# Attention and routed experts: transposes by row halves, and scores of the next pair ahead of back products

## The chip, the cores and the metric

The kernel runs on one core of one Trainium2 chip. Its engines are TensorE (PE, with its weight loads shown apart as PEld), VectorE (DVE), ScalarE (ACT), GpSimd (POOL) and SyncE (SP, which issues most transfers). The metric is the device time of one execution in microseconds, lower is better. Three executions of the kernel before took 696.68, 697.42 and 697.74 us; the median is 697.42 us.

## What is computed

Block-causal attention for 8 batches of 8 heads, 576 positions and 64 features, and behind it a layer of 8 experts, of which each token uses one:

```
scores = (q @ k.T) / 8             # per batch and head
mask   = row // 64 >= column // 64 # blocks of 64 positions
attn   = softmax(where(mask, scores, -1e9))
x      = (attn @ v)                # heads side by side: 4608 tokens x 512
logits = x @ w_gate + modality_bias[modality_id]
e      = argmax(logits);  gate = softmax(logits)[e]
out    = gate * (relu(x @ w1[e]) @ w2[e])
```

## The kernel before

**Tiling.** Two heads of one batch make a pair; there are 32 pairs. The features of the two heads lie on partitions 0 to 63 and 64 to 127, so that a matmul of one head uses one half of the rows of the PE array. The 576 query rows of a head are nine strips of 64; strip s sees 64(s+1) columns. The work of a pair is cut into named steps, and `emit` (called from `run_slot`) writes a step's instructions:

- `Q` (`scale`): queries times 1/8. `S0` to `S3` (`scores`): the strips' scores into PSUM banks 0 to 5, both heads in one bank. S0 is strip 7 in bank 0, S1 strips 6 and 0 in bank 1.
- `M0` to `M4` (`maxima`): negated row maxima on DVE, for strips (7), (6, 0), (5), (4, 2) and (3, 1, 8). `E0` to `E4` (`exps`): exponentials with row sums on ACT, into the tile `pm`.
- `T0` to `T5` (`transposes`): `pm` is turned on PE, 23 blocks of 128 columns with both heads at once, four blocks to a bank. `C0` to `C5` (`copies`): the banks are copied into `pt`, 0, 1 and 5 by DVE, the others by ACT.
- `V` (`values`): value products into banks `o0` and `b0`. `O` (`turn_out`): ACT copies them out to `ot`. `D` (`inverse`): denominators on DVE (`den`, then a reciprocal).
- `B` (`back`): products that turn the result back to rows and add the router's logits, into `o0` and `b0` again. `Z0`, `Z1` (`rows`): DVE scales them into records (`xr`, `gl`), Z0 from `o0`, Z1 from `b0`.
- `L`: SP loads a later pair's queries and keys.

**Order.** Nothing is scheduled by a planner. The table `ORDER` lists (step, stage); in turn `slot` the step is written for pair `slot - stage`, each engine executes in the order of writing, and semaphores are derived from the tiles' uses. A turn is one pass through `ORDER`. The loop is a pipeline: scores, exponentials and transposes of one pair run together with the value and back products of the pair before it. `LAST` is the list for the final pair.

**Routing.** After each fourth pair (a batch) a list of 20 small steps computes where the batch's tokens go. The `q` entries of `ORDER` pop from that list; most are DVE steps. Two are PE matmuls into `b0` (`total`, `counts`, popped at `qp`), and two are ACT copies of those tables out of `b0` (popped at `qv`). At `M3`, `V` and `B` (`SPOTS`) a scatter of records can be written: an index on DVE (L395) and an indirect transfer on POOL. From turn 19 on POOL also splits expert weights there (a CAST and a subtraction, L591 and L592).

**Experts.** Behind attention, from about 290 us on, PE runs the experts' matmuls; the change doesn't touch them.

The array: a matmul takes a stationary operand, loaded first, and streams a moving one. In a transpose the data is stationary and an identity is the moving operand:

```
pe.transpose(banks[g][0:m, 128 * i : 128 * i + 128], d.pm[:, o : o + m], idf)
```

## Time and profile before

| | |
|---|---|
| median of three executions | 697.42 us |
| profiled execution, time | 696.26 us |
| profiled execution, span | 694.5 us |
| PE busy | 685.5 us (99%) |
| PEld busy | 568.8 us (82%) |
| DVE, ACT, POOL busy | 381.3, 352.0, 187.1 us |
[...]

The span is what the profiler saw of the profiled execution; 1.76 us of its time lie around it. A busy time is the union of an engine's instructions. Matmuls are pipelined, so PE can be shown busy and still wait for a moment; a stage's length is read from the starts of its matmuls. Attention takes the first 290 us of the span, the experts the rest.

### The profile page before, as it was taken

The numbers are of one execution on the slowest core, as the hardware profiler recorded it, in microseconds if no ns is written. First come the engines' busy times: TensorE is split into PE (matmuls) and PEld (weight loads), VectorE is DVE, ScalarE is ACT, GpSimd is POOL, SyncE is SP. The second block draws the span as 40 slices with busy tenths as digits, with TensorE's granted clock in tenths as the row PEclk, the third lists the DMA queues.
The fourth block names the chain that finished last, engine by engine and source line by source line (L and its number), as shares of the span: only waits on it lengthen the run. The fifth ranks groups of instructions, "written<-read, shape, count | busy, mean of one in ns | idle before, by whom it ended". The sixth has DMA issues, their size and how long they took to land. (4 is left out here: it accounts for less than half of the span.)

```text
span 694.5 us, 17615 instructions
## 1 busy us (share of the span) xinstructions
PE 685.5 (99%) x6856; PEld 568.8 (82%) x6856; DVE 381.3 (55%) x1090; ACT 352.0 (51%) x1023; POOL 187.1 (27%) x234
## 2 busy tenths in 40 slices
PE   8999999999999999999999999999999999999996
PEld 5888888888888878988888888888888888888885
DVE  6888989999999999883142323223132132322121
ACT  6889899989999898422141322313123032231221
POOL 4000031335275773699311300302002020020201
PEclk9999999999999999999999999999999999999999
DMA  6343354557555763423662520504408040020200
GB/s 223 119 120 117 120 161 145 166 166 220 149 189 212 218 215 114 95 81 113 120 142 92 118 65 1 121 1 105 135 1 242 1 106 15 1 83 1 70 22 19
DMA packets 48070, 76.47 MB, mean 110 GB/s; under 512 B 9710, under 2 KB 30574, under 8 KB 47984
## 3 DMA queue, kind: packets, MB, share of 16 engines
q1 hardware_dynamic: 41456, 55.81, 29.6%
q0 software_dynamic: 6528, 19.50, 7.8%
q8 instruction: 55, 0.90, 0.5%
q14 instruction: 31, 0.25, 0.1%
HBM read 54.19 MB, written 21.27 MB: 109 GB/s over the span
## 5 line engine op out<-in xcount | busy, mean ns | idle before, releaser
L745 DVE SCALAR_TENSOR_TENSOR extra<-bank,extra 128x512 fp32r<-128x512 f32 (+1 forms) x72 | 47.6, 662 | 234.5 <-ACT extra L744 234.5
L229 ACT ACTIVATE pm<-bank,nm 128x512 f32<-128x512 f32 (+3 forms) x320 | 156.0, 502 | 22.8 <-DVE nm L216 22.3
L744 ACT ACTIVATE extra<-bank 128x512 fp32r<-128x512 f32 (+1 forms) x72 | 41.4, 575 | 214.8 <-PE bank L741 214.8
L216 DVE TENSOR_REDUCE nm<-bank 128x1 f32<-128x512 f32 (+3 forms) x320 | 120.5, 446 | 0.7 <-PE bank L209 0.7
L396 POOL DMA_INDIRECT records<-xr,pi x72 | 73.0, 1014 | 174.9 <-DVE pi L395 70.2
L236 PE MATMUL bank<-cf,pm 128*128 128x128 f32 (+1 forms) x736 | 88.7, 276 | 1.9 <-ACT pm L229 1.8
L209 PE MATMUL bank<-raw 64*64 64x512 f32 (+7 forms) x1280 | 87.5, 406 | 0.0
L236 PEld LDWEIGHTS bank<-cf,pm 128*128 128x128 f32 (+1 forms) x736 | 78.6, 139 | 9.0 <-ACT pm L229 7.3
L209 PEld LDWEIGHTS bank<-raw 64*64 64x64 f32 x1280 | 54.6, 133 | 27.9 <-issue 21.5
L259 PE MATMUL b<-pt,v 64*64 64x64 f32 (+1 forms) x868 | 72.7, 265 | 0.0
L259 PE MATMUL o<-pt,v 64*64 64x64 f32 (+1 forms) x868 | 67.2, 261 | 0.0
L241 DVE COPY pt<-bank 128x512 f32<-128x512 f32 (+1 forms) x96 | 58.7, 637 | 14.9 <-PE bank L236 6.5
L229 ACT ACTIVATION_READ_ACCUMULATOR pm<-bank,nm 128x1 f32 x320 | 65.3, 204 | 0.0
L741 PE MATMUL bank<-extra,w0ha 128*128 128x512 f32 (+1 forms) x192 | 62.4, 356 | 0.0
L741 PE MATMUL bank<-extra,w0la 128*128 128x512 f32 (+1 forms) x160 | 58.8, 368 | 0.0
L259 PEld LDWEIGHTS b<-pt,v 64*64 64x64 f32 (+1 forms) x868 | 53.1, 136 | 2.4
L850 POOL DMA_INDIRECT out<-scratch,ids_b x9 | 8.7, 972 | 162.2 <-ACT scratch L849 161.3
L259 PEld LDWEIGHTS o<-pt,v 64*64 64x64 f32 (+1 forms) x868 | 48.4, 135 | 4.4
L241 ACT COPY pt<-bank 128x512 f32<-128x512 f32 x96 | 51.8, 638 | 0.0
L842 PE MATMUL bank<-extra 128*128 128x512 f32 x216 | 50.4, 389 | 0.0
L741 PE MATMUL bank<-xtl,w0ha 128*128 128x512 f32 x128 | 50.0, 390 | 0.0
L741 PE MATMUL bank<-extra,w0hb 128*128 128x512 f32 x128 | 49.8, 389 | 0.0
(235 smaller groups left out, 1147.2 us busy)
## 6 DMA issues: line engine op xcount, KB each, us to landing
raw<-qk SPq DMA_DIRECT2D x31, 576.0 KB, 3.9
v<-vr SPq DMA_DIRECT2D x32, 384.0 KB, 4.0
xr<-records SPq DMA_DIRECT2D x32, 256.0 KB, 5.3
staging<-w SPq DMA_DIRECT2D x32, 128.0 KB, 3.8
staging<-w SPq DMA_DIRECT2D x8, 512.0 KB, 5.0
plain<-w SPq DMA_DIRECT2D x16, 128.0 KB, 6.0
plain<-w SPq DMA_DIRECT2D x4, 512.0 KB, 9.8
records<-bias SPq DMA_DIRECT2D x3, 544.0 KB, 3.5
```

Of the source, the lines that this page charges most:

```text
L209: pe.matmul(place(s, a, b)[64 * t : 64 * t + 64], d.q[hs, D * s : D * s + D], d.k[hs, a:b], start=True, stop=True)
L216: dve.tensor_reduce(d.nm[:, i : i + 1], place(s, a, b), AX.X, ALU.max, negate=True)
L229: act.activation(d.pm[:, o : o + b - a], place(s, a, b), AF.Exp, bias=d.nm[:, s : s + 1], scale=1.0, accum_out=total)
L236: pe.transpose(banks[g][0:m, 128 * i : 128 * i + 128], d.pm[:, o : o + m], idf)
L241: dve.tensor_copy(dst, src) if g in ON_DVE else act.copy(dst, src)
L259: pe.matmul(o.rearrange("p (n c) -> p n c", c=64), d.v[rows, h, block, :], x, start=start, stop=stop)
L396: last = pool.indirect_dma_start(records[:], bass.IndirectOffsetOnAxis(ap=g.pi[i], axis=0), xr[:, i, :], None, bounds_check=2 * NROW - 1, ...
L741: nc.tensor.matmul(hp, w[:, kc, ms], x[:, kc, 0:n], start=i == 0, stop=i == len(mm) - 1)
L744: nc.scalar.activation(hh, hp, AF.Relu)
L745: nc.vector.scalar_tensor_tensor(hl, hp, 0.0, hh, ALU.max, ALU.subtract)
L842: nc.tensor.matmul(y, s.hs[m][x][:, ts], self.part(w, 1, m // 2)[:, m % 2, :], start=first, stop=last)
L850: last = nc.gpsimd.indirect_dma_start(self.out, bass.IndirectOffsetOnAxis(ap=s.list.ids[:, s.t + i : s.t + i + 1], axis=0), yo, None, boun ...
```

## The change

1. **Transposes by halves.** Each of the 23 blocks is turned by two instructions, one for each head: 64 rows of `pm`, 128 columns, against a 64 x 64 identity. Head 0 goes to an even bank and head 1 to the odd bank beside it. There are three groups of 8, 8 and 7 blocks (`GROUPS`) instead of six of four; T0 fills banks 0 and 1, T1 banks 2 and 3, T2 banks 4 and 5. C0 and C1 wait for T0, C2 and C3 for T1, C4 and C5 for T2. A copy moves 512 (C4 and C5: 448) columns and writes runs of 64 into `pt`. The column offsets in `pm` (`OFF`, `TAIL`) are moved so that a half block of strip 2 can be read as a full one. The first group takes blocks of strips 7, 6, 5, 4 and 2.
2. **Order.** S0, S1, M0 and M1 of the next pair are written at the end of a turn, the scores ahead of `B`, the maxima behind it; Z0 and Z1 move from the end of a turn into the next one, Z0 behind M1 and ahead of M2, Z1 behind M2 and ahead of M3. `qv` (the tables' way out) moves behind Z1. `OPENING` writes the first pair's S0, S1, M0 and M1 ahead of the first turn.
3. **Queries.** GpSimd scales the queries of pairs 1 to 17 (`BY_POOL`), where it did pair 1 alone; ACT keeps the later ones.

```diff
--- before.py
+++ after.py
@@ -34,6 +34,7 @@
 COVER = SLOT * NSLOT
 COVER_B = COVER - FEW
 EARLY, NLEAD, LENT = 3, 3, 5
+BY_POOL = 17
 HURRIED = (25, 26, 29, 30, 31)
 LEAD = SLOT * NLEAD
 BIG = float(1 << 20)
@@ -52,14 +53,18 @@
 LONG = (5, 384)
 FLIP = (6, 0, 5, 4, 2)
 PIECES = (((7, 0, 512),), ((6, 0, 448), (0, 0, 64)), ((5, 0, 384), (8, 0, 512)), ((4, 0, 320), (3, 0, 256), (2, 0, 192), (8, 512, 576), (1, 0, 128)))
-OFF = {7: 0, 5: 512, 3: 896, 1: 1152, 6: 1280, 0: 1728, 4: 1792, 8: 2176, 2: 2688}
-TAIL = 2112
+OFF = {7: 0, 5: 512, 3: 896, 1: 1152, 6: 1280, 0: 1728, 2: 1792, 4: 1984, 8: 2368}
+TAIL = 2304
 GROUPS = (
-    ((7, 0), (7, 1), (7, 2), (7, 3)), ((2, 0), (4, 0), (6, 0), (5, 0)), ((3, 0), (3, 1), (6, 2), (5, 2)),
-    ((1, 0), (4, 1), (6, 1), (5, 1)), ((8, 0), (8, 1), (8, 2), (8, 3)), ((6, 3), (4, 2), (2, 1)),
+    ((7, 0), (7, 1), (7, 2), (7, 3), (6, 0), (5, 0), (4, 0), (2, 0)),
+    ((6, 1), (6, 2), (5, 1), (5, 2), (4, 1), (3, 0), (3, 1), (1, 0)),
+    ((6, 3), (4, 2), (2, 1), (8, 0), (8, 1), (8, 2), (8, 3)),
 )
-BLOCK = (12, 0, 8, 4, 16, 20)
-POS = {x: BLOCK[g] + i for g, group in enumerate(GROUPS) for i, x in enumerate(group)}
+ROOMS = (
+    ((2, 0), (4, 0), (6, 0), (5, 0)), ((1, 0), (4, 1), (6, 1), (5, 1)), ((3, 0), (3, 1), (6, 2), (5, 2)),
+    ((7, 0), (7, 1), (7, 2), (7, 3)), ((8, 0), (8, 1), (8, 2), (8, 3)), ((6, 3), (4, 2), (2, 1)),
+)
+POS = {x: 4 * r + i for r, room in enumerate(ROOMS) for i, x in enumerate(room)}
 ON_DVE = (0, 1, 5)
 SUMS = ((2, 4, 6, 5), (1, 3, 7, 8, 0))
 TAILS = ((6, 3, 20, 0), (0, 5, 20, 1), (4, 2, 21, 0), (8, 4, 21, 1), (2, 1, 22, 0))
@@ -69,18 +74,20 @@
 PARTS = (("idf", (128,)), ("ii", (128,)), ("iom8", (NE,)), ("iom72", (NSUB, NE)), ("first9", (NE, NSUB)), ("base8", (NE,)), ("edges", (N // SLOT,)), ("side", (NSUB,)), ("token", (NSUB,)), ("nth", (N // 128,)), ("few", (2,)), ("half", (1,)))
 
 ORDER = (
-    ("S0", 0), ("S1", 0), ("Q", -1), ("M0", 0), ("qv", 1), ("E0", 0), ("S2", 0), ("M1", 0), ("E1", 0), ("S3", 0), ("M2", 0), ("E2", 0), ("M3", 0), ("E3", 0), ("M4", 0),
+    ("Q", -1), ("E0", 0), ("S2", 0), ("Z0", 2), ("M2", 0), ("E1", 0), ("S3", 0), ("Z1", 2), ("qv", 1), ("M3", 0), ("E2", 0), ("M4", 0), ("E3", 0),
     ("L", -2), ("V", 1), ("q1", 1), ("E4", 0), ("O", 1), ("q2", 1), ("q3", 1), ("q4", 1),
-    ("T0", 0), ("C0", 0), ("T1", 0), ("C1", 0), ("D", 1), ("T2", 0), ("C2", 0), ("q5", 1), ("T3", 0), ("C3", 0), ("T4", 0), ("C4", 0), ("T5", 0), ("C5", 0), ("qp", 1), ("B", 1), ("q6", 1), ("Z0", 1), ("Z1", 1),
+    ("T0", 0), ("C0", 0), ("C1", 0), ("D", 1), ("T1", 0), ("C2", 0), ("q5", 1), ("C3", 0), ("T2", 0), ("C4", 0), ("C5", 0),
+    ("S0", -1), ("S1", -1), ("qp", 1), ("B", 1), ("q6", 1), ("M0", -1), ("M1", -1),
 )
+OPENING = ("S0", "S1", "M0", "M1")
 
 SPOTS = ("M3", "V", "B")
 EARLY_STEPS = {
     **{(slot, name): ("prep",) for slot in range(19, 30) for name in SPOTS if (slot, name) != (29, "B")},
-    (18, "S0"): ("chosen",), (18, "V"): ("stage",), (18, "T3"): ("stage",), **{(slot, "T3"): ("restage",) for slot in range(19, 32)}, (20, "L"): ("ids",), (26, "T0"): ("fetch",), (31, "T0"): ("fetch",),
+    (18, "V"): ("chosen", "stage"), (18, "T1"): ("stage",), **{(slot, "T1"): ("restage",) for slot in range(19, 32)}, (20, "L"): ("ids",), (26, "T0"): ("fetch",), (31, "T0"): ("fetch",),
 }
 LAST = (
-    ("+turn0", 0), ("V", 1), ("+place", 0), ("O", 1), ("D", 1), ("+up0", 0), ("+place", 0), ("B", 1), ("Z0", 1), ("Z1", 1), ("+steps1", 0), ("+place", 0), ("+up1", 0),
+    ("Z0", 2), ("Z1", 2), ("+turn0", 0), ("V", 1), ("+place", 0), ("O", 1), ("D", 1), ("+up0", 0), ("+place", 0), ("B", 1), ("Z0", 1), ("Z1", 1), ("+steps1", 0), ("+place", 0), ("+up1", 0),
     ("+place", 0), ("+steps10", 0), ("+place", 0), ("+up2", 0), ("+place", 0), ("+steps9", 0), ("+up3", 0), ("+flush", 0),
 )
 
@@ -185,7 +192,7 @@
         if p == 0:
             for i, j in ((FIRST, S), (0, FIRST)):
                 dve.tensor_scalar(d.q[:, i:j], d.q[:, i:j], SCALE, None, ALU.mult)
-        elif p == 1:
+        elif p <= BY_POOL:
             pool.tensor_scalar(d.q, d.q, SCALE, None, ALU.mult)
         else:
             act.mul(d.q, d.q, SCALE)
@@ -230,15 +237,22 @@
 
     def transposes(p, g):
         d = pairs[p]
-        for i, (s, j) in enumerate(GROUPS[g]):
-            o = OFF[s] + 128 * j
-            m = 64 if s == 2 and j == 1 else 128
-            pe.transpose(banks[g][0:m, 128 * i : 128 * i + 128], d.pm[:, o : o + m], idf)
-
-    def copies(p, g):
+        order = sorted(GROUPS[g], key=POS.get)
+        for s, j in GROUPS[g]:
+            i, o = order.index((s, j)), OFF[s] + 128 * j
+            for h in range(2):
+                hs = slice(64 * h, 64 * h + 64)
+                pe.transpose(banks[2 * g + h][:, 64 * i : 64 * i + 64], d.pm[hs, o : o + 128], idf[hs, hs])
+
+    def copies(p, c):
+        g, h = c // 2, c % 2
         n = len(GROUPS[g])
-        dst, src = pairs[p].pt[:, BLOCK[g] : BLOCK[g] + n].rearrange("p b c -> p (b c)"), banks[g][:, 0 : 128 * n]
-        dve.tensor_copy(dst, src) if g in ON_DVE else act.copy(dst, src)
+        first = min(POS[x] for x in GROUPS[g])
+        dst, src = pairs[p].pt[:, first : first + n, 64 * h : 64 * h + 64], banks[c][:, 0 : 64 * n].rearrange("p (b q) -> p b q", q=64)
+        if g == 0:
+            dst = pairs[p].pt[:, 0:16, 64 * h : 64 * h + 64].rearrange("p (a b) q -> p a b q", b=4)[:, 0:4:3]
+            src = src.rearrange("p (a b) q -> p a b q", a=2)
+        dve.tensor_copy(dst, src) if c in ON_DVE else act.copy(dst, src)
 
     def sides(p):
         return (o0, b0) if p < NPAIR - 1 else (banks[0], banks[1])
@@ -534,6 +548,8 @@
         load(1)
         scale(0)
         load_rest()
+        for name in OPENING:
+            emit(name, 0)
         for slot in range(NPAIR + 1):
             run_slot(slot)
     with tc.manual_schedule(engines=engines):
```

On DVE, at the end of the turn in which the first batch's routing begins (`pt` copies, denominators, then the rows and maxima). Before:

```order
L241 COPY pt1_115<-bank0_97 128x512
L241 COPY pt1_115<-bank1_98 128x512
L286 SCALAR_TENSOR_TENSOR den_851<-sums_635,long0_65 128x9
L287 RECIPROCAL inv_852<-den_851 128x9
L241 COPY pt1_115<-bank5_102 128x384
L299 TENSOR_TENSOR xr1_81<-o0_103,inv_852 128x5x64
L300 TENSOR_TENSOR gl_893<-o0_103,inv_852 128x40
L299 TENSOR_TENSOR xr1_81<-b0_104,inv_852 128x4x64
L300 TENSOR_TENSOR gl_893<-b0_104,inv_852 128x32
L216 TENSOR_REDUCE nm_899<-bank0_97 128x1
L216 TENSOR_REDUCE nm_899<-bank1_98 128x1 x2
L216 TENSOR_REDUCE nm_899<-bank2_99 128x1
```

On DVE, the same place after:

```order
L255 COPY pt1_115<-bank0_97 128x2x4x64
L255 COPY pt1_115<-bank1_98 128x2x4x64
L300 SCALAR_TENSOR_TENSOR den_974<-sums_725,long0_65 128x9
L301 RECIPROCAL inv_975<-den_974 128x9
L255 COPY pt1_115<-bank5_102 128x7x64
L223 TENSOR_REDUCE nm_1012<-bank0_97 128x1
L223 TENSOR_REDUCE nm_1012<-bank1_98 128x1 x2
L313 TENSOR_TENSOR xr1_81<-o0_103,inv_975 128x5x64
L314 TENSOR_TENSOR gl_1049<-o0_103,inv_975 128x40
L223 TENSOR_REDUCE nm_1012<-bank2_99 128x1
L313 TENSOR_TENSOR xr1_81<-b0_104,inv_975 128x4x64
L314 TENSOR_TENSOR gl_1049<-b0_104,inv_975 128x32
```

The rows of a pair (`xr`, `gl`) stood ahead of all maxima (`nm`) and now stand between them.

On PE, in the same turn, from the last transposes to the scores; L323 is the routing table `total`, L280 the back products, L209 the scores. Before:

```order
L236 MATMUL bank5_102<-cf_61,pm1_113 128x128 x2
L236 MATMUL bank5_102<-cf_61,pm1_113 64x128
L323 MATMUL b0_104<-l0_833,cf_61 128x72
L280 MATMUL o0_103<-bk_62,ot_108 64x72 x2
L280 MATMUL b0_104<-bk_62,ot_108 64x72 x2
```

On PE, the same place after (L337 is `total`, L294 the back products, L216 the scores):

```order
L245 MATMUL bank4_101<-cf_61,pm1_113 128x64
L245 MATMUL bank5_102<-cf_61,pm1_113 128x64
L216 MATMUL bank0_97<-raw0_106 64x512 x2
L216 MATMUL bank1_98<-raw0_106 64x448 x2
L216 MATMUL bank1_98<-raw0_106 64x64 x2
L337 MATMUL b0_104<-l0_948,cf_61 128x72
L294 MATMUL o0_103<-bk_62,ot_108 64x72 x2
L294 MATMUL b0_104<-bk_62,ot_108 64x72 x2
```

The first scores of the next pair now stand between the transposes and the back products, and the table stands between the scores and the back products.

## Rows read from the trace of the kernel before

**Rows 1.** The page: the span, and each engine's busy time.
```profile
span 694.5 us, 17615 instructions
...
PE 685.5 (99%) x6856; PEld 568.8 (82%) x6856; DVE 381.3 (55%) x1090; ACT 352.0 (51%) x1023; POOL 187.1 (27%) x234
```

**Rows 2.** Windows: length, busy of PE, PEld, DVE, ACT, POOL (count), clock, DMA, GB/s.
```profile
38.02:46.57 8.55, 8.55 (x165) 7.13 (x161) 6.96 (x21) 7.62 (x27) 0.00 (x0) 1.00 0.39 117
...
115.69:124.42 8.73, 8.73 (x167) 7.44 (x163) 7.73 (x26) 7.80 (x27) 2.03 (x2) 1.00 0.45 146
202.35:211.02 8.67, 8.67 (x167) 7.32 (x163) 8.36 (x29) 7.77 (x28) 6.39 (x9) 1.00 0.63 209
300.00:600.00 300.00, 300.00 (x1324) 248.11 (x1323) 90.25 (x151) 74.16 (x117) 60.85 (x67) 1.00 0.33 84
```

**Rows 3.** Timeline of PE in one turn: start us, length us, instruction, shapes, count.
```profile
37.91 0.60 PE L209 MATMUL bank<-raw 64*64 64x512 f32 x2
...
38.02 2.61 PE L209 MATMUL bank<-raw 64*64 64x448 f32 x38
40.40 0.22 PE L259 MATMUL o<-pt,v 64*64 64x64 f32 x1
...
43.24 2.73 PE L236 MATMUL bank<-cf,pm 128*128 128x128 f32 x23
45.90 0.28 PE L280 MATMUL o<-bk,ot 64*64 64x72 f32 x2
```

**Rows 4.** Timeline of DVE in the same turn.
```profile
38.29 0.49 DVE L299 TENSOR_TENSOR xr<-o,inv 128x320 f32<-128x320 f32 x1 [0.21 <-PE o L280]
...
39.14 0.21 DVE L300 TENSOR_TENSOR gl<-b,inv 128x32 f32<-128x32 f32 x1
39.24 3.73 DVE L216 TENSOR_REDUCE nm<-bank 128x1 f32<-128x512 f32 x10
...
44.00 1.29 DVE L241 COPY pt<-bank 128x512 f32<-128x512 f32 x2 [0.84 <-ACT pm L229]
...
45.40 0.21 DVE L287 RECIPROCAL inv<-den 128x9 f32<-128x9 f32 x1
46.08 0.56 DVE L241 COPY pt<-bank 128x384 f32<-128x384 f32 x1 [0.46 <-ACT pt L241]
```

**Rows 5.** Groups of DVE by form in that turn: busy us, mean ns; the longest reduce and the shortest.
```profile
L216 DVE TENSOR_REDUCE nm<-bank 128x1 f32<-128x512 f32 x2 | 1.4, 681 | 0.0
...
L216 DVE TENSOR_REDUCE nm<-bank 128x1 f32<-128x64 f32 x2 | 0.4, 215 | 0.0
```

**Rows 6.** Timeline of ACT in that turn.
```profile
39.95 0.69 ACT L229 ACTIVATE pm<-bank,nm 128x512 f32<-128x512 f32 x1 [0.93 <-DVE nm L216]
...
46.83 0.75 ACT L191 ACTIVATE raw<-raw 128x576 f32<-128x576 f32 x1
```

**Rows 7.** Weight loads of the transposes: two after a wait, and their lengths (min/median/max ns).
```profile
148.95 0.20 PEld L236 LDWEIGHTS bank<-cf,pm 128*128 128x128 f32 x2 [0.16 <-ACT pm L229]
...
L236 PEld LDWEIGHTS bank<-cf,pm x736: 110/141/143, 7.4 to 280.0; 128*128 128x128 f32 x176, 128*64 128x64 f32 x8
```

**Rows 8.** A turn with a routing table: PE, DVE and ACT timelines.
```profile
54.36 0.34 PE L323 MATMUL b<-l,cf 128*128 128x72 f32 x2
...
56.42 0.20 DVE L300 TENSOR_TENSOR gl<-b,inv 128x32 f32<-128x32 f32 x1
...
56.72 0.22 ACT L327 COPY table<-b 128x72 f32<-128x72 f32 x1 [0.59 <-DVE gl L300]
```

**Rows 9.** DVE's small maxima beside work of POOL: timelines.
```profile
8.75 1.68 POOL L189 TENSOR_SCALAR raw<-raw 128x576 f32<-128x576 f32 x1 [6.66 <-DMA raw<-qk]
...
9.65 0.16 DVE L218 TENSOR_TENSOR nm<-nm 128x1 f32<-128x1 f32 x1
...
207.41 0.72 POOL L592 TENSOR_TENSOR w0la<-staging,w0ha 128x256 fp32r<-128x256 f32 x1
...
207.58 0.56 DVE L218 TENSOR_TENSOR nm<-nm 128x1 f32<-128x1 f32 x1
```

## The prediction

> **What bounds the kernel now.** I read the busy shares first [rows 1], then the same stretches turn by turn [rows 2], then one turn of attention engine by engine [rows 3 to 6]. PE is busy 99% of the span [rows 1], but a busy PE is not proof, so the turn has to show it. A turn (one pair of heads) without routing work takes 8.55 us and PE is busy in all of it, while DVE has 6.96 us and ACT 7.62 us of work [rows 2]. In the PE rows of that turn each stage starts where the last one ends: scores at 38.02, value products at 40.40, transposes at 43.24, back products at 45.90 [rows 3], and the turn ends at 46.57 [rows 2]. DVE waits in the same turn, 0.84 us for the exponentials and 0.46 us before its last copy [rows 4]. So attention is bound by PE's own length, with 0.9 to 1.6 us of slack on ACT and DVE, and little of it late: DVE is busy 7.73 to 8.36 us in turns that carry routing steps [rows 2]. Behind about 290 us the experts' matmuls keep PE full [rows 2]; the change leaves them alone, so a turn saved or lost in attention arrives at the end one for one. [...]
>
> **Part 1, transposes.** Before, 23 full transposes take 2.73 us, (2.73-0.27)/22 = 0.11 us each [rows 3]. After, they are 46 with half the rows and 64 moving columns. If the two halves run side by side, a pair of them costs half a full stream, 0.055 us, or the time of loading 128 columns, whichever is longer: two loads that began at 148.95 ended 0.20 us later, one takes 0.14, so they stand 0.06 us apart [rows 7]. Side by side is what the score matmuls show: the 448-column ones start at 38.02, while 512-column ones that began at 37.91 run until 38.51 [rows 3], in other quarters of the array. I take 0.06 us a pair, 23 x 0.06 = 1.4 us, so PE loses 2.5-1.4 = 1.1 us a turn. The bounds are 0.055 (side by side, stream) and 0.11 to 0.12 (one after the other). PE's own work would come to 8.55-1.1 = 7.4 us.
>
> **Part 2, the order makes a ring.** This decides the case. Before, the rows of a pair (Z0, Z1) are taken before the next maxima and the value products find everything ready. Now DVE runs copies C0, C1, denominators, C5, then M0, M1, Z0, M2, Z1; the value products V overwrite the bank that Z1 reads, so PE stops until Z1 is done; then come V, the first eight transposed pairs, and C0 again. Every link is waited for by the next, and one trip is one turn:
> - M0 to Z1 on DVE: a reduce of 512 columns takes 0.68 us and one of 64 takes 0.215 [rows 5], so 1.04 ns for each column more. The ten of a turn have 2880 columns, 10 x 0.215 + 2240 x 0.00104 = 4.48 us, and lie in 3.73 us [rows 4], a factor 0.83. M0, M1 and M2 are 512, 448, 64 and 384 columns: 4 x 0.215 + 1152 x 0.00104 = 2.06, times 0.83 = 1.71 us. Z0 and Z1 take 38.29 to 39.24, 0.95, and the last one's end lies 0.11 behind the next start. Sum 2.77.
> - DVE to PE: no row shows this hop. DVE to ACT is 0.03 (M0's 0.68 from 39.24 end at 39.92, ACT starts 39.95), PE to DVE 0.11 (transposes end 45.97, copy starts 46.08) [rows 3 to 6]. I take 0.05.
> - V: 40.40 to 43.24, 2.84 [rows 3], less 0.06 for the first matmuls, which don't wait: 2.78.
> - T0: a load 0.06, seven more pairs 0.42, the last record 0.22 (as 64-column matmuls have), hop 0.11: 0.81.
> - C0, C1, denominators: 44.00 to 45.40, 1.40. From the reciprocal to the next start 0.13 to 0.21. C5 with 448 instead of 384 columns 0.62, less 0.08 overlap: 0.54 [rows 4]. Sum 2.07 to 2.15.
> The ring is 8.48 to 8.56 us. Where the instructions overlap a little better than these sums, it is less; 8.35 is my lower bound (0.1 less on V and T0 and 0.05 on DVE). I take 8.45, 0.1 us under the turn of before. PE's 1.1 us becomes waiting.
>
> **Part 3, routing in the ring.** Routing steps on DVE stand at q5 and q6 and the scatter index just before M0, all inside the ring; before they lay in DVE's slack. DVE's work grows from 6.96 to 7.7 us and more in such turns [rows 2], and three of the nine places lie in the ring, so I charge a tenth: 0.1 us a turn on average.
> In half of the turns PE also makes a routing table (`total`, `counts`). Before, it stood behind the transposes in the same mode of the array: turns of 8.73 and 8.67 instead of 8.55 [rows 2], and its two matmuls lie in 0.34 us [rows 8]. Now it stands between the scores of the next pair and the back products. Both use quarters of the array, so they overlap in other turns; here the scores must end, the mode changes twice, and only then the back products run. From C0's start: S1 waits for C1 (1.29), lasts about 0.9, change and table 0.4, back products 0.62+0.22, hop 0.11, so Z0 can start at 3.55; in a turn without table DVE gets there at 2.1+1.26 = 3.37. That is 0.2 us. Then ACT copies the table out only when Z1 is done (Z1 starts 56.42, copy 56.72, 0.22 long [rows 8]), and V waits for that copy too: 0.10+0.22+0.03 = 0.35 us more. So such a turn is 8.45+0.1+0.55 = 9.1 us against 8.7 before. In before the copy lay ahead of exponentials that had time to spare.
> [...]
>
> **Part 4, GpSimd scales queries.** ACT loses 0.75 us for 16 pairs [rows 6], off the ring: nothing. GpSimd needs 1.68 us [rows 9], a turn ahead of its use, and is idle in the early turns [rows 2]: nothing, unless it holds up DVE. Maxima in a late turn took 0.56 instead of 0.16 us while GpSimd subtracted; while it scaled, 0.16 [rows 9]. I take 0.
> The head and tail only shift: the first scores come a stage earlier, and the last pair has no next scores to hide its copies. I set both against each other.
>
> **Sum.** Some 14 turns without a table: 8.45+0.1 against 8.55, nothing. Some 14 with one: 9.1 less 8.7, 0.36 to 0.4, together +5.0 us. The profiled run took 696.26 us (span 694.5); the median of before is 697.42, so 702.4.
>
> **Rivals.**
> - *The ring is shorter and the change pays* (faster). With the lower bounds, 8.3 us a turn, and ACT's table copy hidden, the turns gain 0.25 and 0.1 us: 14 x 0.35 = 5 us, 692.5. For it: DVE and ACT are not full early on [rows 2]. Against: the sum of the links above. Chance 0.27. That PE stays the bound at 7.4 us would need V not to wait for Z1 and is left out.
> - *It cancels* (no change): ring at 8.35 and tables at 0.15 a turn. 697. Chance 0.12.
> - *GpSimd holds DVE up* (slower). The scaling starts when the queries land, some 4 us behind the scores, and so covers the denominators in the ring. Blocked to its end they lose up to 0.8 us in the eight turns before scatters set another rhythm: 8 x 0.8 = 6.4 on top, 708.8. It decides if den takes over 0.5 us there. Against: the 0.16 us [rows 9], one case. Chance 0.08.
> [...]
> - *The halves don't run side by side*, or a load takes 0.11 us: then T takes 2.5 us again, the next scores end later than C5, and the ring grows by 0.7 to 1.0 us: 31 x 0.8 = 25, 727. Against: rows 3 and 7. Chance 0.06. [...]
>
> **Chances.** The forecast has 0.47. Slower by over 0.2% (1.4 us, about what can be told from no change) 0.61, the same 0.12, faster 0.27. The range leaves out the last rival and the ends of the others: 693 to 710.
>
> **What would show it.** PE: transposes in two banks at a time, 23 pairs in about 1.6 us; PE idle ahead of L273 with Z1's L314 or the table's copy as releaser, and of DVE's C0 behind PE. Turns of 8.4 to 8.6 us without and 9.0 to 9.2 with a table. den (L300) at 0.16 us next to a scaling GpSimd. I am wrong if turns fall under 8.3, if V never waits, if pairs of transposes stand 0.1 us apart, or if the granted clock leaves 1.00.

## Result: 1.009 times the time of before

The changed kernel takes **703.67 us** (median of 4 runs, 702.63 to 704.4), the kernel before 697.3 us (median of 4): ratio 1.0091, 95% interval 1.0073 to 1.0108. The profiled run took 702.63 us, its span is 700.9 us.

The page of the changed kernel, its span and the busy time of each engine:

```profile
span 700.9 us, 19050 instructions
...
PE 678.1 (97%) x7592; PEld 551.0 (79%) x7592; DVE 384.3 (55%) x1090; ACT 344.8 (49%) x1007; POOL 213.7 (30%) x250
```

Windows of the changed kernel (length, busy of PE, PEld, DVE, ACT, POOL with counts, clock, DMA share, GB/s): turn 4, without a table; turn 6, with a table; turn 1; and a stretch of the experts:

```profile
38.17:46.57 8.40, 8.21 (x180) 6.58 (x178) 6.89 (x21) 7.20 (x27) 1.71 (x2) 1.00 0.39 124
54.97:64.15 9.18, 8.72 (x184) 6.83 (x181) 7.86 (x25) 7.69 (x29) 2.29 (x2) 1.00 0.33 105
12.53:21.07 8.54, 8.52 (x145) 6.29 (x146) 5.96 (x15) 6.33 (x24) 2.46 (x2) 0.86 0.36 115
300.00:600.00 300.00, 299.90 (x1337) 248.89 (x1337) 94.56 (x176) 75.23 (x121) 66.00 (x71) 1.00 0.33 85
```

Against [rows 2]: a turn without a table fell from 8.55 to 8.40 us, one with a table rose from 8.73 to 9.18, the experts' stretch is as full as it was. PE still counts as busy in 8.21 of 8.40 us although 1.1 us of its work is gone: the ends of matmuls are modelled, so that a short wait shows as busy, and a gap under 0.15 us gets no bracket. The waits and the starts tell more. They stand in the timeline of PE of the changed kernel (start, length, instruction, count, idle time before it and who ended it): two rows of turn 4, one of turn 6, one of the transposes in a later turn, and three of the tail:

```profile
41.75 0.27 PE L273 MATMUL b<-pt,v 64*64 64x64 f32 x2 [0.20 <-DVE gl L314]
...
44.48 1.78 PE L245 MATMUL bank<-cf,pm 64*128 64x64 f32 x46
...
59.33 0.27 PE L273 MATMUL b<-pt,v 64*64 64x64 f32 x2 [0.46 <-ACT table L341]
...
97.29 1.65 PE L245 MATMUL bank<-cf,pm 64*128 64x64 f32 x46
...
281.57 0.27 PE L273 MATMUL b<-pt,v 64*64 64x64 f32 x2 [0.54 <-ACT table L345]
...
287.21 2.90 PE L273 MATMUL bank<-pt,v 64*64 64x64 f32 x56 [0.49 <-DVE pt L255]
290.05 0.38 PE L757 MATMUL bank<-extra,w0ha 128*128 128x256 f32 x1
```

The timeline of DVE of the changed kernel, turn 4, and below it three rows of turn 6:

```profile
38.92 1.35 DVE L223 TENSOR_REDUCE nm<-bank 128x1 f32<-128x512 f32 x3
40.19 0.48 DVE L313 TENSOR_TENSOR xr<-o,inv 128x320 f32<-128x320 f32 x1
...
41.49 0.20 DVE L314 TENSOR_TENSOR gl<-b,inv 128x32 f32<-128x32 f32 x1
...
45.23 1.29 DVE L255 COPY pt<-bank 128x512 f32<-128x512 f32 x2 [1.44 <-PE bank L245]
46.43 0.16 DVE L300 SCALAR_TENSOR_TENSOR den<-sums,long 128x9 f32<-128x9 f32 x1
...
55.72 1.35 DVE L223 TENSOR_REDUCE nm<-bank 128x1 f32<-128x512 f32 x3
57.30 0.49 DVE L313 TENSOR_TENSOR xr<-o,inv 128x320 f32<-128x320 f32 x1 [0.23 <-issue]
...
58.77 0.20 DVE L314 TENSOR_TENSOR gl<-b,inv 128x32 f32<-128x32 f32 x1
```

**The ring, link by link.** M0 starts at 38.92, Z1 ends at 41.69: 2.77 us. The value products start 0.06 later (41.75, waiting for L314, which is Z1) and last until 44.48: 2.73. From the first transpose to C0 at 45.23: 0.75. From C0 to the next M0 (38.92+8.40 = 47.32): 2.09. Sum 8.40, the turn. PE waits for DVE's Z1, DVE waits 1.44 us for PE's transposes, and the turn closes.

**A table in the ring.** Turn 6 is 0.78 us longer than turn 4, and three links hold all of it: from M0 to Z0 1.58 instead of 1.27 us, from Z0 to the end of Z1 1.67 instead of 1.50, from there to the value products 0.36 instead of 0.06. The last is the table's copy; the first two, 0.48 together, come with the table's place on PE ahead of the back products.

**Where the 6.4 us went.** The experts' first matmul starts at 290.05 instead of 283.95, 6.10 later; the two spans differ by 6.4. Turn by turn (from the first 448-column score product of a turn to that of the next), turns 2 to 30 contain 13 with a table, mean 9.21 us, and 16 without, mean 8.53; before they were 14 with, mean 8.72, and 15 without, mean 8.63. So 13 x 9.21 + 16 x 8.53 - 14 x 8.72 - 15 x 8.63 = 4.7 us. Turns 0 and 1 give 0.2, the tail from the start of the last pair's scores to the experts 12.75 instead of 11.50: 1.25.

### The profile page after: what moved, and what is told of

It reads as the page before. It is cut to its first block, busy times and chain, and to the rows that moved or that the text cites. A ratio compares the mean times of both kernels' runs of the same rounds, so it can differ in the third digit from the quotient of the medians.

```text
span 700.9 us, 19050 instructions
## 1 busy us (share of the span) xinstructions
PE 678.1 (97%) x7592; PEld 551.0 (79%) x7592; DVE 384.3 (55%) x1090; ACT 344.8 (49%) x1007; POOL 213.7 (30%) x250
## 5 line engine op out<-in xcount | busy, mean ns | idle before, releaser
L223 DVE TENSOR_REDUCE nm<-bank 128x1 f32<-128x512 f32 (+3 forms) x320 | 124.8, 450 | 2.5 <-PE bank L216 2.2
L216 PE MATMUL bank<-raw 64*64 64x64 f32 (+7 forms) x1280 | 106.4, 414 | 0.4 <-DVE pt L255 0.4
L216 PEld LDWEIGHTS bank<-raw 64*64 64x64 f32 x1280 | 60.8, 134 | 37.3 <-issue 22.2
L273 PE MATMUL o<-pt,v 64*64 64x64 f32 (+1 forms) x868 | 73.3, 264 | 0.0
L273 PEld LDWEIGHTS b<-pt,v 64*64 64x64 f32 (+1 forms) x868 | 48.5, 136 | 19.0 <-ACT table L345 5.0
L245 PE MATMUL bank<-cf,pm 64*128 64x64 f32 x1472 | 58.2, 227 | 1.6 <-ACT pm L236 0.9
L245 PEld LDWEIGHTS bank<-cf,pm 64*128 64x128 f32 x1472 | 51.8, 139 | 9.1 <-ACT pm L236 5.3
L273 PEld LDWEIGHTS o<-pt,v 64*64 64x64 f32 (+1 forms) x868 | 50.3, 135 | 4.4
L255 ACT COPY pt<-bank 128x512 f32<-128x512 f32 (+1 forms) x96 | 49.8, 608 | 0.0
L757 PE MATMUL bank<-extra,w0lb 128*128 128x512 f32 x128 | 49.8, 389 | 0.0
```

The lines of the kernel that those rows point to most:

```text
L216: pe.matmul(place(s, a, b)[64 * t : 64 * t + 64], d.q[hs, D * s : D * s + D], d.k[hs, a:b], start=True, stop=True)
L223: dve.tensor_reduce(d.nm[:, i : i + 1], place(s, a, b), AX.X, ALU.max, negate=True)
L245: pe.transpose(banks[2 * g + h][:, 64 * i : 64 * i + 64], d.pm[hs, o : o + 128], idf[hs, hs])
L255: dve.tensor_copy(dst, src) if c in ON_DVE else act.copy(dst, src)
L273: pe.matmul(o.rearrange("p (n c) -> p n c", c=64), d.v[rows, h, block, :], x, start=start, stop=stop)
L757: nc.tensor.matmul(hp, w[:, kc, ms], x[:, kc, 0:n], start=i == 0, stop=i == len(mm) - 1)
```

## The same program in another set of runs

Each set of experiments ran on one chip, with the kernel before beside it. The first two sets (order, halves, act, qve; again, zz, zz_qve, ring_in) fell on one chip, here A; base, spots and best on a chip B, qp_qve on a chip C. Which chip the result's set ran on is not recorded. Before took 696.7 to 697.4 us (medians) in all sets. The changed kernel did not take the same everywhere, so it was run again, unchanged:

> The changed kernel itself, unchanged, beside the others of this call. In the runs with ACT's scaling and with the earlier table copy the first copy of a turn on DVE stood 0.3 to 0.8 us later than the last transpose it needs, in every turn in which GpSimd issues scatters late in the turn, and nowhere else. If that delay belongs to those two edits: 703.7 us here, and no such delay. If it does not (it comes and goes between sets of runs with one and the same program): about 717 us, with delays of 0.3 to 0.8 us in the some 18 turns with scatters.

Measured on A: **718.56 us** (717.26 to 719.47), ratio 1.0306 (1.0288 to 1.0324), 15 us more than the same program had taken in the result. So the delay does not belong to the edits of act and qve. Turn 21 has scatters and no table. C0 is DVE's first copy there. Timelines of GpSimd, DVE and PE there, first the changed kernel in the result's run:

```profile
194.78 1.00 POOL L410 DMA_INDIRECT records<-xr,pi  x1 [0.36 <-DVE pi L409]
...
195.30 1.29 DVE L255 COPY pt<-bank 128x512 f32<-128x512 f32 x2 [0.43 <-issue]
...
194.55 1.85 PE L245 MATMUL bank<-cf,pm 64*128 64x64 f32 x46
```

The same three timelines of the same turn in the run "again", on chip A:

```profile
202.26 1.01 POOL L410 DMA_INDIRECT records<-xr,pi  x1 [0.36 <-DVE pi L409]
...
203.60 1.29 DVE L255 COPY pt<-bank 128x512 f32<-128x512 f32 x2 [1.25 <-PE bank L245]
...
202.03 1.86 PE L245 MATMUL bank<-cf,pm 64*128 64x64 f32 x46
```

C0 starts 0.75 us behind the first transpose in the one, 1.57 in the other, 0.33 behind the end of GpSimd's scatter issue (203.27). In the run on A there are 18 turns in which C0 comes due inside such an issue or just behind it: in all 18 it starts 0.30 to 0.56 us after the issue's end, and in 16 of them later behind its transposes than in the result's run, which has its issues at the same places (in turns 15 and 26 the two runs agree within 0.01 us). In the 13 other turns from turn 1 on it is never late. The record multiplies (Z0, L313) are late on A in the same way: DVE idles 0.42 to 0.84 us ahead of them in 18 turns, at most 0.17 in the result's run in a turn with scatters. I call this the hold.

**What is late is PE's signal, not DVE.** The kept trace also has the times at which an engine's semaphore counts up. In turn 4 PE's count for the third of the transposes that C0 needs comes 0.27 us after their start, and C0 starts with it; so it is in every turn from turn 1 on without an issue nearby, on A and in the result's run. In turn 21 on A the same count comes 1.09 us after their start, at 203.61, C0 starts at 203.60, and ACT's first copy, which waits for PE too, starts with its own count, at 203.81. Over all issues on A the middle delay from the start of a matmul to its count is 0.61 us, against 0.24 elsewhere in that run and 0.24 beside the issues of the result's run; DVE's and ACT's own counts keep their 0.01 us beside issues as elsewhere (middle values). So DVE is free and waits for PE. Why PE's counts, or the writes behind them, come late is open, and so is why only in these two sets: that it is the chip fits them, and the sets on B and C without it, but was not tried by itself.

Turns 2 to 8 have no scatter, and the changed kernel's sum over them is the same in both sets (so is that of before, in its two); that block is where kernels can be compared across sets:

```
sums of turns, us           time     turns 2-8    turns 9-30
before, result's set       697.3      60.29        191.25
base (before), chip B      697.78     60.29        191.24
after, result's set        703.67     60.62        195.62
again (after), chip A      718.56     60.63        210.78
act, A                     718.55     60.63        210.77
qve, A                     717.06     60.15        210.00
zz, A                      709.98     59.11        203.20
zz_qve, A                  709.30     58.75        203.04
ring_in, A                 727.78     64.09        213.66
order, A                   730.35     66.20        217.29
halves, A                  699.72     58.50        194.62
spots, B                   702.94     60.68        195.55
best, B                    696.88     58.79        190.87
qp_qve, C                  700.52     60.00        193.96
```

Of the 16.7 us between the two profiled spans of the changed kernel (700.9 and 717.6), turns 9 to 30 hold 15.2. In the result's run C0, whose input is a bank in PSUM, starts inside the issue (195.30, the issue runs from 194.78 to 195.78); on A (203.60) it starts with PE's count.

## Experiments on the change's parts

**The order alone.** Before's groups and full transposes, in the new order:

```diff
-    ("S0", 0), ("S1", 0), ("Q", -1), ("M0", 0), ("qv", 1), ("E0", 0), ("S2", 0), ("M1", 0), ("E1", 0), ("S3", 0), ("M2", 0), ("E2", 0), ("M3", 0), ("E3", 0), ("M4", 0),
+    ("Q", -1), ("E0", 0), ("S2", 0), ("Z0", 2), ("M2", 0), ("E1", 0), ("S3", 0), ("Z1", 2), ("qv", 1), ("M3", 0), ("E2", 0), ("M4", 0), ("E3", 0),
...
-    ("T0", 0), ("C0", 0), ("T1", 0), ("C1", 0), ("D", 1), ("T2", 0), ("C2", 0), ("q5", 1), ("T3", 0), ("C3", 0), ("T4", 0), ("C4", 0), ("T5", 0), ("C5", 0), ("qp", 1), ("B", 1), ("q6", 1), ("Z0", 1), ("Z1", 1),
+    ("T0", 0), ("C0", 0), ("T1", 0), ("C1", 0), ("D", 1), ("T2", 0), ("C2", 0), ("q5", 1), ("T3", 0), ("C3", 0), ("T4", 0), ("C4", 0), ("T5", 0), ("C5", 0),
+    ("S0", -1), ("S1", -1), ("qp", 1), ("B", 1), ("q6", 1), ("M0", -1), ("M1", -1),
 )
+OPENING = ("S0", "S1", "M0", "M1")
...
```

> The new order alone, with the 23 full transposes and six groups of before and GpSimd scaling pair 1 only. Ring theory: the trip through DVE and PE is as long as in the changed kernel, and the full transposes lie in it, so a turn is 9.2 to 9.3 us without a routing table and 9.6 to 9.7 with one, and the whole about 724 us (715 to 730). Rival, the order costs nothing by itself and the loss comes from the halves or from GpSimd: 697 us, turns of 8.55 and 8.7.

Measured: 730.35 us, ratio 1.0481 (1.0464 to 1.0499). Turn 4 takes 9.35 us, turn 6 with a table 9.76. PE's wait for Z1 is there as in the changed kernel, with the 2.73 us of full transposes behind it. Timelines of order in turn 4, two rows of PE and one of DVE:

```profile
43.82 0.27 PE L261 MATMUL b<-pt,v 64*64 64x64 f32 x2 [0.54 <-DVE gl L302]
...
46.55 2.73 PE L238 MATMUL bank<-cf,pm 128*128 128x128 f32 x23
...
40.99 1.35 DVE L218 TENSOR_REDUCE nm<-bank 128x1 f32<-128x512 f32 x3 [0.39 <-PE bank L211]
```

The order costs 0.8 us a turn by itself; the rival is out. The time lies above the 724 forecast, at the end of its range, and this run has the hold in its later turns; what it would take without was not run.

**The halves alone.** The changed kernel's transposes and copies in before's ORDER with the new T and C units, ACT scaling the queries again, and no opening:

```diff
-BY_POOL = 17
+BY_POOL = 1
...
-    ("Q", -1), ("E0", 0), ("S2", 0), ("Z0", 2), ("M2", 0), ("E1", 0), ("S3", 0), ("Z1", 2), ("qv", 1), ("M3", 0), ("E2", 0), ("M4", 0), ("E3", 0),
+    ("S0", 0), ("S1", 0), ("Q", -1), ("M0", 0), ("qv", 1), ("E0", 0), ("S2", 0), ("M1", 0), ("E1", 0), ("S3", 0), ("M2", 0), ("E2", 0), ("M3", 0), ("E3", 0), ("M4", 0),
...
-    ("T0", 0), ("C0", 0), ("C1", 0), ("D", 1), ("T1", 0), ("C2", 0), ("q5", 1), ("C3", 0), ("T2", 0), ("C4", 0), ("C5", 0),
-    ("S0", -1), ("S1", -1), ("qp", 1), ("B", 1), ("q6", 1), ("M0", -1), ("M1", -1),
+    ("T0", 0), ("C0", 0), ("C1", 0), ("D", 1), ("T1", 0), ("C2", 0), ("q5", 1), ("C3", 0), ("T2", 0), ("C4", 0), ("C5", 0), ("qp", 1), ("B", 1), ("q6", 1), ("Z0", 1), ("Z1", 1),
 )
-OPENING = ("S0", "S1", "M0", "M1")
+OPENING = ()
...
```

> Transposes by halves alone, in the order of before (first scores and maxima at the start of a turn, rows behind the back products), GpSimd scaling pair 1 only. Ring theory: PE loses 1.1 us a turn, but from about 8.2 us on the trip DVE, ACT, PE of the old order sets the turn; turns of 8.15 to 8.25 without and about 8.4 with a table, 688 to 692 us. Rival, PE's own time sets the turn: turns of 7.5 us, 664 us. Rival, the halves do not run side by side: 697 us or more.

Measured: 699.72 us, ratio 1.0042 (1.0028 to 1.0056); turn 4 takes 8.23 us, as the ring theory said, and not 7.5. So PE's saving alone gives 0.32 us a turn, and what is late next is the old order's own trip, on ACT and DVE. Timelines of halves in turn 4, ACT and PE:

```profile
40.22 0.69 ACT L235 ACTIVATE pm<-bank,nm 128x512 f32<-128x512 f32 x1 [0.67 <-DVE nm L222]
...
44.96 0.94 PE L244 MATMUL bank<-cf,pm 64*128 64x64 f32 x14 [0.25 <-ACT pm L235]
```

The last transposes wait for the exponentials, the back products and Z0, Z1, M0 stand behind them, and the exponentials wait for M0. The whole is 8 us above the forecast of 688 to 692. Turns 2 to 8 gave their 1.8 us (60.29 to 58.50); turns 9 to 30 lost 3.4, with C0 late next to scatter issues (in turn 9 it starts 1.75 us behind its first transposes and 0.43 behind an issue's end). What it would take without the hold was not run.

**GpSimd's scaling.** ACT scales the queries of pairs 2 to 17 again:

```diff
-BY_POOL = 17
+BY_POOL = 1
```

> The changed kernel with ACT scaling the queries of pairs 2 and on, as before. Ring theory: ACT has the time, 703.7 us as in the changed kernel, within 1 us. Rival, GpSimd's scaling holds up DVE's denominators: 5 to 6 us come back, 698 us.

Measured on A: 718.55 us, against 718.56 for the changed kernel there; turns 2 to 8 60.63 in both. The scaling costs nothing here and gives nothing. In the result's run the denominators took 0.16 us (46.43 above) while GpSimd scaled, as its timeline there shows:

```profile
45.50 1.65 POOL L196 TENSOR_SCALAR raw<-raw 128x576 f32<-128x576 f32 x1 [6.69 <-DMA raw<-qk]
```

That is a matter of timing. In the nine turns of that run in which the denominators lie beside a scaling they start 0.51 to 1.49 us behind its start, and take 0.16 or 0.17 us. Where a moved step brings them to 0.04 to 0.46 us behind that start they end 0.69 us behind it and take 0.23 to 0.65 us: eight times in qve, zz, zz_qve, best and qp_qve. DVE and GpSimd in the run qve (below):

```profile
55.46 0.61 DVE L300 SCALAR_TENSOR_TENSOR den<-sums,long 128x9 f32<-128x9 f32 x1
...
55.38 1.65 POOL L196 TENSOR_SCALAR raw<-raw 128x576 f32<-128x576 f32 x1 [7.50 <-PE bank L245]
```

**The table's way out.** The copy moved behind the first exponential:

```diff
-    ("Q", -1), ("E0", 0), ("S2", 0), ("Z0", 2), ("M2", 0), ("E1", 0), ("S3", 0), ("Z1", 2), ("qv", 1), ("M3", 0), ("E2", 0), ("M4", 0), ("E3", 0),
+    ("Q", -1), ("E0", 0), ("qv", 1), ("S2", 0), ("Z0", 2), ("M2", 0), ("E1", 0), ("S3", 0), ("Z1", 2), ("M3", 0), ("E2", 0), ("M4", 0), ("E3", 0),
```

> The changed kernel with one step moved: the copy of the routing table out of PSUM comes on ACT behind the first exponential of a turn, not behind the sixth. Theory: in the 15 turns with a table the value products wait for that copy; without that wait these turns fall from 9.1 to about 8.75 us, and the time from 703.7 to about 699 us; turns without a table stay at 8.4 to 8.5. Rival, the price of a table is PE's change of mode and the late start of the back products alone: 703.7 us, unchanged.

Measured on A: 717.06 us, 1.5 less than the changed kernel there. Turns 6 and 8 go from 9.19 and 9.07 to 8.97 and 8.80: 0.22 and 0.27 for the copy, not 0.35. PE's wait in turn 6 changes its releaser, from the copy (0.46, above) to Z1, in the timeline of PE of qve:

```profile
59.74 0.27 PE L273 MATMUL b<-pt,v 64*64 64x64 f32 x2 [0.25 <-DVE gl L314]
```

Of the eleven later turns with a table the three without an issue at C0 gain 0.27 to 0.30 us, the other eight nearly nothing: their value products start earlier too (0.25 in turn 10), but C0 still starts behind the issue's end, 1.11 instead of 0.89 us behind its transposes in turn 10.

**Both ends of the table.** The copy as above, and PE's matmuls (qp) ahead of the scores:

```diff
-    ("Q", -1), ("E0", 0), ("S2", 0), ("Z0", 2), ("M2", 0), ("E1", 0), ("S3", 0), ("Z1", 2), ("qv", 1), ("M3", 0), ("E2", 0), ("M4", 0), ("E3", 0),
+    ("Q", -1), ("E0", 0), ("qv", 1), ("S2", 0), ("Z0", 2), ("M2", 0), ("E1", 0), ("S3", 0), ("Z1", 2), ("M3", 0), ("E2", 0), ("M4", 0), ("E3", 0),
...
-    ("S0", -1), ("S1", -1), ("qp", 1), ("B", 1), ("q6", 1), ("M0", -1), ("M1", -1),
+    ("qp", 1), ("S0", -1), ("S1", -1), ("B", 1), ("q6", 1), ("M0", -1), ("M1", -1),
```

> The changed kernel with both ends of the routing table moved: its two matmuls stand behind the last transposes again, ahead of the next pair's scores, and its copy behind the first exponential. Theory of two prices (the back products wait for scores and two changes of mode, and the value products wait for the copy): turns 6 and 8, which have a table and no scatter, go from 9.18 and 9.07 us to 8.5 to 8.65, where the earlier copy alone gave 8.97 and 8.80; turns without a table stay at 8.40 to 8.47; in all 6 to 8 us less than the changed kernel: 696 to 698 us where its time is 703, 711 to 713 us where it is 718.6. Rival, the copy was the whole price: 8.97 and 8.80 again, 701 to 702 us or 717.

Measured on C, where there is no hold: 700.52 us, ratio 1.005 (1.0033 to 1.0067), 3.2 less than the result's 703.67, not 6 to 8. Turns 6 and 8: 8.86 and 8.68, not 8.5 to 8.65. The matmuls now delay the scores, and M0 waits for those. Timelines of qp_qve in turn 6, DVE and PE:

```profile
55.66 1.35 DVE L223 TENSOR_REDUCE nm<-bank 128x1 f32<-128x512 f32 x3 [0.37 <-PE bank L216]
...
58.58 0.27 PE L273 MATMUL b<-pt,v 64*64 64x64 f32 x2 [0.64 <-DVE gl L314]
```

So both theories fall short. The copy is 0.22 to 0.30 of the price, and neither place tried for PE's side takes it away: ahead of the scores it is paid at M0, behind them at Z0.

**More work inside the ring.** One more reduce of 512 columns on DVE in `maxima`, ahead of M1:

```diff
-            d.nm = sml.tile([128, NSUB + 1], F32, name="nm")
+            d.nm = sml.tile([128, NSUB + 2], F32, name="nm")
...
+        if u == 1:
+            dve.tensor_reduce(d.nm[:, NSUB + 1 : NSUB + 2], place(7, 0, 512), AX.X, ALU.max, negate=True)
```

> The changed kernel with one more reduce of 512 columns on DVE ahead of M1 in every turn (its result goes to a column that nobody reads), 0.58 us inside the trip. Ring theory: turns without a table grow by 0.45 to 0.6 us, those with one by 0.1 to 0.5 (there the back products end late), 9 to 15 us more than the changed kernel beside it. Rival, PE or ACT sets the turn and DVE has slack (6.9 us busy of 8.4): under 2 us.

Measured on A: 727.78 us, 9.2 more than the changed kernel there. Turn 4 grows by 0.60 us, from 8.40 to 9.00, for a reduce of 0.6, while DVE is busy in 7.49 of it, as the window of ring_in shows (columns as above):

```profile
41.58:50.58 9.00, 8.43 (x180) 6.57 (x178) 7.49 (x22) 7.15 (x27) 1.71 (x3) 1.00 0.40 127
```

DVE's idle 1.5 us is no slack. The extra reduce also delays the first exponential (ACT waits 1.14 us there), so this run does not say which trip through DVE it is.

**Less work inside the ring.** Z1 ahead of M2:

```diff
-    ("Q", -1), ("E0", 0), ("S2", 0), ("Z0", 2), ("M2", 0), ("E1", 0), ("S3", 0), ("Z1", 2), ("qv", 1), ("M3", 0), ("E2", 0), ("M4", 0), ("E3", 0),
+    ("Q", -1), ("E0", 0), ("S2", 0), ("Z0", 2), ("Z1", 2), ("M2", 0), ("E1", 0), ("S3", 0), ("qv", 1), ("M3", 0), ("E2", 0), ("M4", 0), ("E3", 0),
```

> The changed kernel with Z1 moved ahead of M2 (Z0, Z1, M2 instead of Z0, M2, Z1). Ring theory: one reduce of 384 columns (0.46 us) leaves the trip from DVE's C0 to the value products, so a turn without a table falls from 8.4 to 8.0 to 8.25 us (from there on the exponentials set it) and one with a table from 9.1 to about 8.6; 8 to 11 us less than the changed kernel beside it. Rival, the turn is set elsewhere (ACT or PE): less than 2 us difference.

Measured on A: 709.98 us, 8.6 less than the changed kernel there, but not from where it was expected: turn 4 still takes 8.40 us. What fell are the turns with a table (turns 6 and 8: 8.61 and 8.69) and turns with scatters (turn 21: 8.24 instead of 9.34, where C0 now comes due just as the issue begins). In turn 4 PE still starts the products for Z1's bank when Z1 is done (42.22, with Z1's end at 42.16; the weight load shows the wait, 0.23 instead of 0.33 us, the matmul's is too short for a bracket). But that no longer sets the turn; another trip is just as long. Timelines of zz in turn 4, two rows each of DVE and ACT, PE's weight loads, and two rows of PE:

```profile
39.85 1.35 DVE L223 TENSOR_REDUCE nm<-bank 128x1 f32<-128x512 f32 x3 [0.32 <-PE bank L216]
...
42.05 2.47 DVE L223 TENSOR_REDUCE nm<-bank 128x1 f32<-128x384 f32 x7
...
40.58 0.69 ACT L236 ACTIVATE pm<-bank,nm 128x512 f32<-128x512 f32 x1 [0.48 <-DVE nm L223]
...
44.62 0.47 ACT L236 ACTIVATE pm<-bank,nm 128x256 f32<-128x256 f32 x1 [0.24 <-PE o L273]
...
42.22 0.14 PEld L273 LDWEIGHTS b<-pt,v 64*64 64x64 f32 x2 [0.23 <-DVE gl L314]
...
42.22 0.27 PE L273 MATMUL b<-pt,v 64*64 64x64 f32 x2
...
44.95 2.25 PE L245 MATMUL bank<-cf,pm 64*128 64x64 f32 x46
```

The transposes take 2.25 us instead of 1.78, because the last of them wait for the exponentials; S0 stands behind them on PE, and M0 waits 0.32 for S0. The second trip, link by link: DVE works without a pause from M0 (39.85) to the last maximum (44.52); E4 starts 0.10 later, 0.08 behind DVE's count as in the changed kernel (the row names PE, whose count came last); ACT is done with it at 46.50; S0 starts at 47.12, behind the transposes that waited; the next M0 at 48.25. Sum 8.40. Z0 and Z1 lie in this trip wherever they stand between M0 and M4, so moving Z1 could not shorten it. In the changed kernel it is there too: the transposes of turn 4 take 1.78 us and not 1.65. So the ring of the prediction was a bound that held, beside a second one as long within 0.01 us, which it did not see.

**Both moves.** Z1 ahead of M2 and the copy behind E0:

```diff
-    ("Q", -1), ("E0", 0), ("S2", 0), ("Z0", 2), ("M2", 0), ("E1", 0), ("S3", 0), ("Z1", 2), ("qv", 1), ("M3", 0), ("E2", 0), ("M4", 0), ("E3", 0),
+    ("Q", -1), ("E0", 0), ("qv", 1), ("S2", 0), ("Z0", 2), ("Z1", 2), ("M2", 0), ("E1", 0), ("S3", 0), ("M3", 0), ("E2", 0), ("M4", 0), ("E3", 0),
```

> The changed kernel with both moves: Z1 ahead of M2, and the copy of the table behind the first exponential. Ring theory: turns of 8.1 to 8.3 us with and without a table, 9 to 12 us less than the changed kernel beside it. Rival, only one of the two waits was real: no better than the run with Z1 alone by more than 1 us, or no better than the changed kernel.

Measured on A: 709.30 us, 9.3 less than the changed kernel there, 0.7 less than with Z1 alone. The turns stay above the 8.1 to 8.3 us expected: a plain one takes 8.40, as with Z1 alone, and turns 6 and 8 8.49 and 8.40. In the whole the rival's mark (not over 1 us better than Z1 alone) is met, but in turns 6 and 8 the copy does take off 0.12 and 0.29 us more (8.61 and 8.69 with Z1 alone), so both waits were real. Turns 2 to 8 sum to 58.75, against 60.29 before; turns 9 to 30, with the hold, to 203.04, against 191.25.

**Before, traced on chip B.**

> The kernel before, for a trace taken beside the runs of the experiments. Theory: the hold is there too (a copy or a record multiply of DVE that falls into an indirect DMA issue of GpSimd starts 0.4 to 0.8 us behind its end), but DVE's first copy has over 1 us until PE wants the bank, so turns with scatters stay at 8.55 to 8.9 us and the time at 697. Rival, no such hold in this program: DVE's copies start with their transposes as in the first trace.

Measured: 697.78 us, and no hold: C0 starts at 96.80, in the middle of the issue from 96.34 to 97.32. Timelines of base, GpSimd and DVE:

```profile
96.34 0.98 POOL L396 DMA_INDIRECT records<-xr,pi  x1 [1.22 <-DVE lg L334]
...
96.80 1.28 DVE L241 COPY pt<-bank 128x512 f32<-128x512 f32 x2
```

That is what the changed kernel shows in the result's run, so this trace tells nothing of before on chip A. Its time on A, 696.9, says only that a hold, if it is there, costs it nothing.

**A scatter place moved.** `prep`, which issues the scatters, at M4 instead of V:

```diff
-SPOTS = ("M3", "V", "B")
+SPOTS = ("M3", "M4", "B")
```

> The changed kernel with one of the three scatter places of a turn moved, from ahead of the value products to ahead of M4 on DVE: GpSimd's second indirect DMA issue of a turn then ends about 1 us before DVE's first copy is due. Theory, the copy is held while GpSimd issues an indirect DMA: the delays of 0.4 to 0.5 us of that copy vanish in the turns with two scatters, 4 to 8 us less than the 718.6 us of the changed kernel in these sets (711 to 715); the delay of the record multiply Z0, behind the third place, stays. Rival, the delay hangs on something else: within 1.5 us of 718.6.

Measured on B: 702.94 us, ratio 1.0091 (1.0075 to 1.0108), the time of the result. But the edit did not do it: in turn 21 C0 starts inside an issue there too, 0.03 us behind its transposes, and Z0 is not late either. The runs on chip B show no hold, so whether a moved scatter avoids it stays open.

**Three moves together.** Z1 ahead of M2, the copy behind E0, the scatter place:

```diff
-    ("Q", -1), ("E0", 0), ("S2", 0), ("Z0", 2), ("M2", 0), ("E1", 0), ("S3", 0), ("Z1", 2), ("qv", 1), ("M3", 0), ("E2", 0), ("M4", 0), ("E3", 0),
+    ("Q", -1), ("E0", 0), ("qv", 1), ("S2", 0), ("Z0", 2), ("Z1", 2), ("M2", 0), ("E1", 0), ("S3", 0), ("M3", 0), ("E2", 0), ("M4", 0), ("E3", 0),
...
-SPOTS = ("M3", "V", "B")
+SPOTS = ("M3", "M4", "B")
```

> Three moves together: Z1 ahead of M2, the table's copy behind the first exponential, the scatter place ahead of M4. By the ring theory with the hold: turns of 8.1 to 8.4 us without late scatters, 0.5 to 0.8 us less in the turns with two scatters than with the first two moves alone (709.3 us); 698 to 704 us. Rival, the holds only move to another copy: 707 to 710 us.

Measured on B: 696.88 us (10 runs), before beside it 696.74; ratio 1.0 (0.999 to 1.001). That is under the 698 to 704 us forecast, which counted on the hold. Turns 2 to 8 gain 1.5 us on before, turns 9 to 30 0.4, and the head and the tail take that back: the medians differ by 0.1 us. It repairs the change and does not beat before.

## The prediction, point by point

- **The time and its sign**: 702.4 forecast, 703.67 measured. Slower, for the reason given. On chip A the same program took 718.6, beyond the range of 693 to 710, so that the result fell inside it was in part luck of the set. Part of the sum is luck too: plain turns went from 8.63 to 8.53 us on average where nothing was forecast, turns with a table from 8.72 to 9.21 where 0.36 to 0.4 was, and head and tail were left out; the first offsets much of the other two.
- **Part 1, transposes**: right. 46 records lie in 1.65 us; less the last one's 0.27 that is 1.38 for 22 steps, 0.06 us a pair. PE's work fell, and the 1.1 us became waiting.
- **Part 2, the ring**: right in each link (2.77 against 2.77; 0.06 against 0.05; 2.73 against 2.78; 0.75 against 0.81; 2.09 against 2.07 to 2.15), 8.40 against 8.45, which was itself chosen under the 8.48 to 8.56 that the links add up to. (The lower bound, 8.48 less 0.1 and 0.05, is 8.33; and the hop of 0.11 from PE to DVE was read at a copy that by its row waited for ACT.) What it missed is the second trip of the same length (zz): the price of the ring was right, the gain from cutting it would not have been.
- **Part 3, tables and routing**: right in sum, 9.21 on average against 9.1, mis-sized in its terms. The copy cost 0.30 at the value products of turn 6, and moving it gave 0.22 to 0.30, instead of 0.35. Turns without a table carried 0.13 for routing (8.53 against 8.40), near the 0.1 charged. PE's part was 0.48 between M0 and Z1's end instead of 0.2. The change of mode in the 0.4 of "change and table" was the author's estimate, and no run shows it by itself. What turn 6 shows is the order: the last scores start at 55.83, the table's two matmuls at 55.98, the back products at 56.36. In turn 4, without a table, the back products start at 47.39, 0.21 ahead of the end of the last 448-column scores (47.60). Moving PE's part as well as the copy takes off only 0.11 more (8.97 to 8.86), which leaves 0.46 above turn 4's 8.40; M0's wait of 0.37 is the table again. With the copy and Z1 moved, turn 6 takes 8.49 (zz_qve). So the charge of 0.2 us at PE was too small, that for the copy too large.
- **Part 4, GpSimd**: right, nothing (act), as long as the denominators start late enough in the scaling: they took 0.16 or 0.17 us where they started 0.51 us or more behind its start, 0.23 to 0.65 where they started 0.04 to 0.46 behind it.
- **Head and tail**: the step that failed. "I set both against each other" put them at nothing; they cost 0.2 at the head and 1.25 at the tail. At the tail the last pair's value products wait 0.54 for the table's copy and the final ones 0.49 for C copies that no next scores hide, where before they ran through.
- **The clock**: forecast at 1.00 throughout. Turn 1 ran at 0.86, which by the prediction's own list was a sign of being wrong; it touched no other turn. From 11.5 to about 15 us the granted clock was 0.50 to 0.57, instead of 1.00; in the 5 us in which it fell PE was busy for 3.47 (1.25, 1.14 and 1.08 in the first three rows). Windows of the changed kernel, columns as above:

```profile
7.00:9.00 2.00, 1.25 (x26) 0.77 (x18) 2.00 (x8) 2.00 (x9) 0.00 (x0) 1.00 1.02 366
9.00:10.50 1.50, 1.14 (x20) 0.84 (x20) 1.28 (x4) 1.50 (x9) 1.24 (x1) 1.00 1.11 353
10.50:12.00 1.50, 1.08 (x15) 0.69 (x13) 0.92 (x2) 1.50 (x7) 0.43 (x1) 0.82 0.92 373
...
13.00:14.00 1.00, 1.00 (x8) 0.23 (x2) 0.32 (x1) 0.06 (x1) 0.66 (x1) 0.50 0.17 59
14.00:15.00 1.00, 1.00 (x14) 0.54 (x12) 0.46 (x1) 0.00 (x0) 0.98 (x1) 0.57 0.00 0
```

  What set it off stays open: before had PE busy for only 3.23 us of the same 5 us (1.11, 0.62 and 1.50) and stayed at 1.00. The least busy of its windows:

```profile
9.00:10.50 1.50, 0.62 (x5) 0.59 (x6) 1.39 (x4) 1.50 (x8) 1.43 (x1) 1.00 1.06 377
```

  Where it stayed at 1.00 in the changed order (spots) turn 1 took 7.46 instead of 8.54 us, though turn 0 took 8.36 instead of 7.82 there, so the net is 0.5 us.
- **The rivals**: "the ring is shorter", "it cancels" and "halves not side by side" are out by the numbers above. "GpSimd holds DVE up" is out for this kernel's scaling, beside which every den took 0.16 or 0.17 us, and in part borne out elsewhere: den took over 0.5 us in qve, zz and best, where it started within 0.1 us of the scaling, but it ended 0.69 us behind the scaling's start and not at its end (1.65). Beside GpSimd's subtraction (L608, 0.72 us) den took 0.43 to 0.70 us in six turns of the result's run, from turn 19 on, where it started 0.05 to 0.32 us behind the subtraction's start. The 15 us on chip A are another thing: there PE's counts come late beside GpSimd's indirect DMA issues (middle delay 0.61 us instead of 0.24), and DVE waits for PE. No rival had that.
